# Preparing the third dense weight tile ahead of a branch, loading its raw words over GpSimd's queue, and a scheduling fence at the branch

## The chip, the cores and the metric

The kernel runs on one core of a Trainium2 chip. The metric is the device time of one execution in microseconds (us). The engines are named as in the profile: PE (TensorE's matmuls), PEld (its weight loads), DVE (VectorE), ACT (ScalarE), POOL (GpSimd) and SP (SyncE, which issues most transfers). The letter q behind an engine's name means its sequencer, the part that takes instructions in order.

## What is computed

Three stages follow each other. Attention over 4 batches, 8 heads and 576 positions gives `x` of 2304 tokens by 512. A mixture of 8 experts sends each token to one expert. A dense layer with squared ReLU gives the output:

```python
def _moe_ref(x, w_gate, w_output_gate, w1, w2):
    ...
        h = np.maximum(x[mask] @ w1[e], 0.0)
        ye = h @ w2[e]
        out[mask] = gate_w[mask, None] * eom[mask, e, None] * ye
...
def _moe2_ref(x, w_in, w_out):          # x 2304x512, w_in 512x2048, w_out 2048x512
    h = np.maximum(x @ w_in, 0.0)
    return (h * h @ w_out).astype(np.float32)
```

The dense weights `w_in` and `w_out` arrive as float64. The change concerns only how their first tiles reach the dense layer.

## The kernel before

**Numbers as pairs.** The kernel keeps float32 accuracy on the matmul engine by splitting each operand into a rounded part (hi, type fp32r) and a rest (lo). `mm3` issues three matmuls, hi by hi (L79), hi by lo (L80) and lo by hi (L81), into one accumulator.

**The expert stage** works through units of one or two slots of 128 tokens. Units 0 to 15 (`run(0, NU0)`) always run. Four more units (`run(NU0, NU)`) stand behind a branch, `tc.If(state["used"] > NS0)` (L1065), and run only when routing needs more than 22 slots; in this execution it does not, and they are skipped. Each unit takes four weight chunks `raw0` to `raw3` over SP's queue, ACT and DVE (or POOL) split them into `wc`, PE multiplies, and at the unit's end DVE scales each slot's result into a tile `y` (L975), which SP writes to `y_rest` in device memory (L977). There is one `y` tile only (`YB = 1`), so each scaling waits until the write of the one before it is over.

**The dense stage** takes the 18 token blocks in five groups: four of four blocks and one of two. For each group it runs 16 steps f of 128 hidden columns. Step f does 12 matmuls into `phf` (function `l1`: `x @ w_in`), then ACT's ReLU, square and cast (L1163, L1167, L1169) and DVE's subtraction (L1170) make `gT`, and 12 matmuls per step add `gT @ w_out` into `po` (function `l2`, two steps later in group 0). There are two `phf` buffers.

**The dense weights.** `weights(f)` turns the raw 64-bit words of weight tile f, 128 columns of `w_in` and 128 rows of `w_out`, into hi and lo. Raw words come in two transfers of 512 KB (L1089, L1090). Then ACT takes the absolute value (L1093), a maximum follows (L1094; on DVE for tiles 0 and 1, on POOL for the others), DVE does three integer operations (L1095, L1096, L1097), ACT casts hi (L1098) and DVE subtracts lo (L1100). All 16 tiles are made once, during group 0, and stay. Tiles 0 and 1 (`NPRE = 2`) are made in the expert stage by the generator `dense_prep` (called `ahead`), of which `step(u, place)` takes a piece wherever the table `AH` holds that unit and place. The same generator loads the first four blocks of tokens (`ytp`) and transposes them (`pty`).

**Buffers.** The raw words of tiles 0, 1, 2 and 3 and `ytp` take turns in two buffers of tag `fraw` (`NRAW = 2`); tile 4 and later ones use a place called `spare` as well, which is free only behind the expert stage.

**What sets the order.** In the expert stage the code's order is the order of PE, ACT, DVE and POOL (`manual_schedule`); SP's order and the whole dense stage are set when the program is built, by a scheduler which may also move dense work ahead of the branch when it depends on nothing there. When the branch falls through, SP goes through one semaphore wait for each transfer lane before it continues.

Of the kernel before, what the change touches and what calls it, by code (L numbers as in the profile page):

```python
# [20 lines left out]
P = 128  # L21
# [11 lines left out]
NPRE = 2  # L33
GW = P + 32
NRAW = 2
AH = ((3, 0), (3, 2), (3, 2), (3, 2), (3, 2), (2, 0), (2, 2), (2, 2), (1, 1), (1, 1))
HOLD = 10
LAG = 7
RT0 = 5
# [778 lines left out]
def experts(tc, c, st, x_dram, w1, w2, routed, ahead):  # L818
    nc = tc.nc
    e = st.enter_context  # L820
# [241 lines left out]
        man.close()  # L1062

    run(0, NU0)
    with tc.If(state["used"] > NS0):  # L1065
        run(NU0, NU)


def dense_prep(tc, c, st, w_in, w_out):
    nc = tc.nc  # L1070
    e = st.enter_context
    pre = e(tc.tile_pool(name="pre", bufs=1, side="right", reuse_waits="tile"))
    cv = e(tc.tile_pool(name="cv", bufs=2, side="right", reuse_waits="tile"))
    tiny = 2.0 ** -15
    win32 = w_in.bitcast(I32).rearrange("(k p) (f t) -> p k f t", p=P, t=2)
    wout32 = w_out.bitcast(I32).rearrange("r (f t) -> r f t", t=2)
    c.wi, c.wo = {}, {}
    c.yT = {}

    def weights(f, pool):  # L1080
        w = pool.tile([P, 2, 2, 512], F32R, name=f"w{f}")
        c.wi[f] = w[:, :, 0].rearrange("p t (k q) -> p t k q", k=4)
        c.wo[f] = w[:, :, 1]
        hi, lo = (w[:, t].rearrange("p i q -> p (i q)") for t in range(2))
        raw = c.spare[:, f % 2] if f >= 4 and f & 2 == 0 else cv.tile([P, 2, 512, 2], I32, tag="fraw", name="fraw", bufs=NRAW)
        x = (cv if f < NPRE or f % 2 == 0 else pool).tile([P, 1024], I32, tag="x", name="x", bufs=1)
        xf = x.bitcast(F32)
        with tc.issue_after(c.last) if f < NPRE else nullcontext():
            nc.sync.dma_start(out=raw[:, 0].rearrange("p (k f) t -> p k f t", k=4), in_=win32[:, :, f * P:(f + 1) * P, :])  # L1089
            nc.sync.dma_start(out=raw[:, 1], in_=wout32[f * P:(f + 1) * P])  # L1090
        yield
        lw, hw = (raw.rearrange("p i q t -> p (i q) t")[:, :, t] for t in range(2))
        nc.scalar.activation(xf, hw.bitcast(F32), AF.Abs)  # L1093
        c.pmax = (nc.vector if f < NPRE else nc.gpsimd).tensor_scalar_max(xf, xf, tiny)  # L1094
        nc.vector.tensor_scalar(out=x, in0=x, scalar1=0x07FFFFFF, scalar2=3, op0=ALU.bitwise_and, op1=ALU.logical_shift_left)  # L1095
        nc.vector.scalar_tensor_tensor(out=x, in0=lw, scalar=29, in1=x, op0=ALU.logical_shift_right, op1=ALU.bitwise_or)  # L1096
        nc.vector.scalar_tensor_tensor(out=lw, in0=hw, scalar=-1073741824, in1=x, op0=ALU.bitwise_and, op1=ALU.bitwise_or)  # L1097
        nc.scalar.copy(hi, lw.bitcast(F32))  # L1098
        yield
        nc.vector.tensor_sub(lo, lw.bitcast(F32), hi.bitcast(F32))  # L1100
        yield

    c.weights = weights
    c.yTeven = lambda: pre.tile([P, 2, 4, 4, P], F32R, tag="yT", name="yT")
    yT = c.yT[0] = c.yTeven()
    yt = cv.tile([P, 4, DM], F32, tag="fraw", name="ytp", bufs=NRAW)
    for j in range(2):
        with tc.issue_after(c.last):
            nc.sync.dma_start(out=yt[:, 2 * j:2 * j + 2], in_=c.y_first[2 * j * P:(2 * j + 2) * P].rearrange("(i p) f -> p i f", p=P))
    yield  # L1110
    for j in range(4):
        turn(nc, c, c.bank("pty"), yt[:, j], yT[:, :, j])
        if j % 2:
            yield
    conv = [weights(f, pre) for f in range(NPRE)]
    for g in conv:
        yield from g


def turn(nc, c, pt, src, dst):  # L1120
# [7 lines left out]
def dense(tc, c, st, out):  # L1128
    nc = tc.nc
    e = st.enter_context  # L1130
    dg = e(tc.tile_pool(name="dg", bufs=1, reuse_waits="tile"))
    res = e(tc.tile_pool(name="res", bufs=1, reuse_waits="tile"))
    io = e(tc.tile_pool(name="dio", bufs=2, reuse_waits="tile"))
    hb = e(tc.tile_pool(name="dhb", bufs=2, space=PSUM, reuse_waits="tile"))
    pb = e(tc.tile_pool(name="dpb", bufs=2, space=PSUM, reuse_waits="tile"))
    NF = FF // P
# [42 lines left out]
    for g, (b0, nb) in enumerate(groups):  # L1179
# [4 lines left out]
        gts = {}  # L1184
        lag = 1 if g else 2
        for f in range(NF):
            conv = c.weights(f + 2, res) if g == 0 and NPRE <= f + 2 < NF else iter(())
            next(conv, None)
            gts[f] = l1(g, f)
            for _ in conv:  # L1190
                pass
            if f == HOLD and g == 0:
                hold = c.pmax.ins
            if g < len(groups) - 1:
                if f >= lag:
# [123 lines left out]
```

## Time and profile before

| | us |
|---|---|
| median of 3 runs | 927.83 (927.36 to 929.69) |
| the profiled execution, device time | 928.89 |
| its span, first to last instruction | 927.2 |
| mean granted TensorE clock | 0.993 of full speed |
| PE busy | 900.4 (97%) |
| DVE busy | 579.3 (62%) |
| ACT busy | 469.7 (51%) |
| POOL busy | 228.2 (25%) |

The device time exceeds the span by 1.7 us, which lies outside of the instructions. Attention lasts until about 250 us, the last expert matmul of the profiled execution starts at 508.36 us, the dense stage follows, and its group 0 ends at about 610 us. All times in the rows below count from the span's start.

### The profile page before, as it was taken

The numbers are of one execution on the slowest core, as the hardware profiler recorded it, in microseconds if no ns is written. First come the engines' busy times: TensorE is split into PE (matmuls) and PEld (weight loads), VectorE is DVE, ScalarE is ACT, GpSimd is POOL, SyncE is SP. The second block draws the span as 40 slices with busy tenths as digits, with TensorE's granted clock in tenths as the row PEclk, the third lists the DMA queues.
The fourth block names the chain that finished last, engine by engine and source line by source line (L and its number), as shares of the span: only waits on it lengthen the run. The fifth ranks groups of instructions, "written<-read, shape, count | busy, mean of one in ns | idle before, by whom it ended". The sixth has DMA issues, their size and how long they took to land. (4 is left out here: it accounts for less than half of the span.)

```text
span 927.2 us, 14490 instructions
## 1 busy us (share of the span) xinstructions
PE 900.4 (97%) x5212; PEld 725.1 (78%) x5212; DVE 579.3 (62%) x1080; ACT 469.7 (51%) x934; POOL 228.2 (25%) x275
## 2 busy tenths in 40 slices
PE   7999999999999999999999799999999999999996
PEld 4677777876557889989898587788888888888895
DVE  8789989997686887766677699732223222322332
ACT  5888787864444766565563576622222222322231
POOL 6433433322002142154222345420002000100000
PEclk9999999999999999999999999999999999999998
DMA  9887777745548978766734656110002000100000
GB/s 223 217 196 188 198 197 185 175 110 173 193 149 289 354 279 281 268 226 189 263 122 149 215 182 204 46 58 12 12 12 69 12 12 1 45 1 1 12 35 23
DMA packets 83483, 129.23 MB, mean 139 GB/s; under 512 B 9360, under 2 KB 35984, under 8 KB 83408
## 3 DMA queue, kind: packets, MB, share of 16 engines
q1 hardware_dynamic: 78784, 113.31, 40.2%
q0 software_dynamic: 4624, 14.95, 4.9%
q8 instruction: 43, 0.70, 0.3%
q14 instruction: 32, 0.26, 0.1%
HBM read 109.10 MB, written 15.99 MB: 135 GB/s over the span
## 5 line engine op out<-in xcount | busy, mean ns | idle before, releaser
L1165 DVE SCALAR_TENSOR_TENSOR r<-phf,r 128x512 f32<-128x512 f32 (+1 forms) x64 | 40.0, 625 | 176.2 <-ACT r L1163 176.2
L1163 ACT ACTIVATE r<-phf 128x512 f32<-128x512 f32 (+1 forms) x80 | 44.4, 555 | 196.1 <-PE phf L81 182.3
L852 DVE TENSOR_TENSOR wc<-raw,wc 128x1024 fp32r<-128x1024 f32 x91 | 116.0, 1319 | 12.4 <-ACT wc L850 10.9
L79 PE MATMUL phf<-yT,w 128*128 128x512 f32 (+1 forms) x320 | 121.0, 378 | 2.4 <-ACT w L1098 2.2
L81 PE MATMUL phf<-yT,w 128*128 128x512 f32 (+1 forms) x320 | 119.1, 372 | 0.7 <-DVE w L1100 0.5
L80 PE MATMUL phf<-yT,w 128*128 128x512 f32 (+1 forms) x320 | 117.9, 369 | 0.0
L850 ACT CAST wc<-raw 128x1024 fp32r<-128x1024 f32 x108 | 106.4, 1057 | 20.5 <-DMA raw<-in_w_dram 13.7
L79 PE MATMUL po<-w,gT 128*128 128x512 f32 x256 | 100.6, 394 | 2.6 <-ACT gT L1169 2.6
L80 PE MATMUL po<-w,gT 128*128 128x512 f32 x256 | 99.9, 390 | 0.0
L81 PE MATMUL po<-w,gT 128*128 128x512 f32 x256 | 91.0, 391 | 0.0
L252 ACT ACTIVATE a<-sc,negm 128x512 f32<-128x512 f32 (+3 forms) x128 | 67.0, 532 | 16.8 <-DVE negm L249 16.8
L79 PEld LDWEIGHTS phf<-yT,w 128*128 128x128 f32 x320 | 60.2, 188 | 15.6 <-ACT w L1098 3.9
L81 PEld LDWEIGHTS phf<-yT,w 128*128 128x128 f32 x320 | 60.2, 188 | 13.3 <-DVE w L1100 3.2
L79 PE MATMUL py<-wc,hT 128*128 128x512 f32 x176 | 70.0, 397 | 0.3 <-ACT hT L889 0.3
L80 PE MATMUL py<-wc,hT 128*128 128x512 f32 x176 | 68.9, 391 | 0.8 <-DVE wc L852 0.8
L81 PE MATMUL py<-wc,hT 128*128 128x512 f32 x176 | 68.9, 391 | 0.3 <-DVE hT L890 0.3
L852 POOL TENSOR_TENSOR wc<-raw,wc 128x1024 fp32r<-128x1024 f32 x17 | 44.5, 2621 | 97.0 <-ACT wc L850 88.5
L80 PEld LDWEIGHTS phf<-yT,w 128*128 128x128 f32 x320 | 60.3, 189 | 9.7
L1170 DVE TENSOR_TENSOR gT<-r,gT 128x512 fp32r<-128x512 f32 x64 | 44.2, 691 | 34.2 <-ACT gT L1169 33.4
L249 DVE TENSOR_REDUCE negm<-sc 128x1 f32<-128x512 f32 (+3 forms) x128 | 55.6, 478 | 6.9 <-PE sc L246 6.7
L79 PEld LDWEIGHTS po<-w,gT 128*128 128x128 f32 x256 | 48.1, 188 | 13.7 <-ACT gT L1169 3.5
L1169 ACT CAST gT<-r 128x512 fp32r<-128x512 f32 x64 | 39.7, 621 | 33.4 <-DVE r L1165 33.0
(345 smaller groups left out, 2040.0 us busy)
## 6 DMA issues: line engine op xcount, KB each, us to landing
raw<-in_w_dram SPq DMA_DIRECT2D x64, 1024.0 KB
q<-qh SPq DMA_DIRECT2D x60, 128.0 KB
fraw<-in_w_in_dram SPq DMA_DIRECT2D x10, 512.0 KB
fraw<-in_w_out_dram SPq DMA_DIRECT2D x10, 512.0 KB
kraw<-in_k_dram SPq DMA_DIRECT2D x16, 288.0 KB
qraw<-in_q_dram SPq DMA_DIRECT2D x16, 288.0 KB
y_rest<-y SPq DMA_DIRECT2D x17, 256.0 KB
vts<-in_v_dram SPq DMA_DIRECT2D x16, 256.0 KB
```

The costliest lines, as they stand in the source:

```text
L79: nc.tensor.matmul(out, lhsT=lh, rhs=rh, start=start, stop=False)
L80: nc.tensor.matmul(out, lhsT=lh, rhs=rl, start=False, stop=False)
L81: return nc.tensor.matmul(out, lhsT=ll, rhs=rh, start=False, stop=stop)
L249: nc.vector.tensor_reduce(out=negm[:, h, j:j + 1], in_=psv, axis=AX.X, op=ALU.max, negate=True)
L252: nc.scalar.activation(a[:, h, aoff[j]:aoff[j] + nk], psv, AF.Exp, bias=negm[:, h, j:j + 1], accum_out=ssum[:, h, j:j + 1])
L850: nc.scalar.copy(wc[:, 0, ks], raw[:, ks])
L852: eng.tensor_sub(wc[:, 1, ks], raw[:, ks], wc[:, 0, ks].bitcast(F32))
L1163: nc.scalar.activation(r[:, 0:nt], ph[:, 0:nt], AF.Relu)
L1165: nc.vector.scalar_tensor_tensor(out=r[:, 0:nt], in0=ph[:, 0:nt], scalar=0.0, in1=r[:, 0:nt], op0=ALU.max, op1=ALU.mult)
L1169: nc.scalar.copy(gT[:, 0, 0:nt], r[:, 0:nt])
L1170: nc.vector.tensor_sub(gT[:, 1, 0:nt], r[:, 0:nt], gT[:, 0, 0:nt].bitcast(F32))
```

## The change

Tile 2 is prepared ahead of the branch up to its ACT cast, with the maximum on DVE. The raw words of tiles 0, 1 and 2 and the block load `ytp` go out over GpSimd's queue instead of SP's, and are no longer tied to come after the last chunk load (`issue_after`). The table `AH` has 8 entries instead of 10, which also brings the conversion of tile 1 one place forward. Ahead of the branch what is left of the generator is run, and a fence, `tc.no_sync_barrier()`, keeps the scheduler from moving anything that is written behind it to a place before it. The lines of the dense stage move (L1093 to L1097 become L1092 to L1096, L1098 becomes L1103, L1100 becomes L1105).

```diff
-AH = ((3, 0), (3, 2), (3, 2), (3, 2), (3, 2), (2, 0), (2, 2), (2, 2), (1, 1), (1, 1))
+AH = ((3, 0), (3, 2), (3, 2), (3, 2), (2, 0), (2, 1), (2, 2), (1, 0))
...
     run(0, NU0)
+    for _ in ahead:
+        pass
+    tc.no_sync_barrier()
     with tc.If(state["used"] > NS0):
         run(NU0, NU)
...
-    def weights(f, pool):
-        w = pool.tile([P, 2, 2, 512], F32R, name=f"w{f}")
+    def weights(f):
+        raw = c.spare[:, f % 2] if f >= 4 and f & 2 == 0 else cv.tile([P, 2, 512, 2], I32, tag="fraw", name="fraw", bufs=NRAW)
+        x = (cv if f <= NPRE or f % 2 == 0 else c.res).tile([P, 1024], I32, tag="x", name="x", bufs=1)
+        xf = x.bitcast(F32)
+        eng = nc.gpsimd if f <= NPRE else nc.sync
+        eng.dma_start(out=raw[:, 0].rearrange("p (k f) t -> p k f t", k=4), in_=win32[:, :, f * P:(f + 1) * P, :])
+        eng.dma_start(out=raw[:, 1], in_=wout32[f * P:(f + 1) * P])
+        yield
...
+        c.pmax = (nc.vector if f <= NPRE else nc.gpsimd).tensor_scalar_max(xf, xf, tiny)
...
+        if f == NPRE:
+            yield
+        w = (pre if f < NPRE else c.res).tile([P, 2, 2, 512], F32R, name=f"w{f}")
...
-        with tc.issue_after(c.last):
-            nc.sync.dma_start(out=yt[:, 2 * j:2 * j + 2], in_=c.y_first[2 * j * P:(2 * j + 2) * P].rearrange("(i p) f -> p i f", p=P))
+        nc.gpsimd.dma_start(out=yt[:, 2 * j:2 * j + 2], in_=c.y_first[2 * j * P:(2 * j + 2) * P].rearrange("(i p) f -> p i f", p=P))
+    convs = [weights(f) for f in range(NPRE + 1)]
+    next(convs[0])
...
+    next(convs[2])
+    c.begun = convs[2]
+    yield
...
-            conv = c.weights(f + 2, res) if g == 0 and NPRE <= f + 2 < NF else iter(())
+            conv = iter(()) if g or f + 2 >= NF else c.weights(f + 2) if f + 2 > NPRE else c.begun
```

**SP's queue ahead of the branch.** Before the change its last rows are these; `raw3_3709` is the last expert chunk, `fraw_6455` holds tile 1, `fraw_6933` tile 2 and `fraw_6964` tile 3, and the `y` tiles are the slots of the last two units. A bracket lists the semaphores that an instruction waits for.

```order
L842 DMA raw3_3709<-in_w2_dram 128x4x512 [waits DMAHW6_49,DMAHW1_49,DVE_49]
L1089 DMA fraw_6455<-in_w_in_dram 128x4x256 [waits PE_49]
L1090 DMA fraw_6455<-in_w_out_dram 128x1024 [waits DMAHW3_49]
L1089 DMA fraw_6933<-in_w_in_dram 128x4x256 [waits DMAHW4_49]
L1090 DMA fraw_6933<-in_w_out_dram 128x1024 [waits DMAHW5_49]
L977 DMA y_rest_62<-y_6448 128x512 [waits DVE_49]
L977 DMA y_rest_62<-y_6451 128x512 [waits DMAHW7_49,DVE_49]
L1089 DMA fraw_6964<-in_w_in_dram 128x4x256 [waits DMAHW2_49,DMAHW3_49,DMAHW0_49,DVE_49]
L1090 DMA fraw_6964<-in_w_out_dram 128x1024 [waits DMAHW1_49]
L977 DMA y_rest_62<-y_6516 128x512 [waits DVE_49]
L977 DMA y_rest_62<-y_6519 128x512 [waits DVE_49]
L1065 COMPARE_AND_BRANCH
```

After the change the same stretch reads so:

```order
L842 DMA raw3_3709<-in_w2_dram 128x4x512 [waits DMAHW5_49,DMAHW2_49,DVE_49]
L977 DMA y_rest_62<-y_6463 128x512 [waits DMAHW6_49,DVE_49]
L977 DMA y_rest_62<-y_6466 128x512 [waits DMAHW7_49,DVE_49]
L977 DMA y_rest_62<-y_6525 128x512 [waits DVE_49]
L977 DMA y_rest_62<-y_6528 128x512 [waits DMAHW1_49,DVE_49]
L1088 DMA fraw_6964<-in_w_in_dram 128x4x256 [waits DMASW3_49,DMASW4_49,DMASW0_49,DMASW7_49,PE_49,Activation_49]
L1089 DMA fraw_6964<-in_w_out_dram 128x1024 [waits DMAHW3_49]
L1068 COMPARE_AND_BRANCH
```

The loads of tiles 1 and 2 have left this queue, and the load of tile 3 has moved from ahead of the last two `y` writes to behind them; it now stands directly at the branch.

**ACT behind the branch.** Before the change, from the last two casts of expert weights to the second ReLU, ACT's rows are these; `phf_6937` is step 0 and `phf_6968` step 1.

```order
L850 CAST wc_6850<-raw3_3709 128x1024 [waits DMAHW0_49,DVE_49,Pool_49]
L850 CAST wc_6850<-raw3_3709 128x1024
L1065 UNCONDITIONAL_BRANCH
L1065 UNCONDITIONAL_BRANCH [waits Activation_49]
L1163 ACTIVATE r_6950<-phf_6937 128x512 [waits DMASW6_49,DMASW5_49,DMASW7_49,DMASW2_49,PE_49]
L1098 CAST w2_6932<-fraw_6933 128x1024 [waits DMAHW2_49,DVE_49,Activation_49]
L1093 ACTIVATE x_6965<-fraw_6964 128x1024 [waits DMAHW0_49,DVE_49,DMAHW1_49,PE_49,DMAHW3_49,Activation_49,Pool_49]
L1167 ACTIVATE r_6950<-r_6950 128x512 [waits Activation_49]
L1169 CAST gT_6953<-r_6950 128x512 [waits DMASW3_49,DMASW4_49,DMASW1_49,DMASW6_49,DMASW0_49,Activation_49]
L1093 ACTIVATE x_6995<-spare_6927 128x1024 [waits DMAHW5_49,DMAHW4_49]
L1163 ACTIVATE r_6981<-phf_6968 128x512 [waits DVE_49]
```

After the change (`phf_6944` is step 0, `fraw_6329` tile 2):

```order
L850 CAST wc_6860<-raw3_3709 128x1024 [waits DMAHW0_49,DVE_49,Pool_49]
L850 CAST wc_6860<-raw3_3709 128x1024
L1068 UNCONDITIONAL_BRANCH
L1068 UNCONDITIONAL_BRANCH [waits Activation_49]
L1103 CAST w2_6942<-fraw_6329 128x1024 [waits DVE_49,DMAHW2_49,PE_49,Activation_49]
L1092 ACTIVATE x_6965<-fraw_6964 128x1024 [waits DVE_49,DMAHW3_49,Activation_49,Pool_49]
L1181 ACTIVATE r_6957<-phf_6944 128x512 [waits DMASW5_49,PE_49]
L1185 ACTIVATE r_6957<-r_6957 128x512 [waits Activation_49]
L1187 CAST gT_6960<-r_6957 128x512 [waits DMASW4_49,DMASW3_49,Activation_49]
L1092 ACTIVATE x_6995<-spare_6937 128x1024 [waits DMAHW5_49,DMAHW4_49]
L1181 ACTIVATE r_6981<-phf_6968 128x512 [waits DVE_49,PE_49]
```

The first ReLU (`r_6957<-phf_6944`) stood first behind the branch; it now stands third, behind the absolute value of tile 3 (`x_6965<-fraw_6964`), which waits for tile 3's raw words (the lane DMAHW3).

**DVE ahead of the branch.** After the change its last rows are these; `x_6257` is tile 1 and `x_6330` tile 2. Before the change the order was `wc`, the first two `y`, all of tile 1, a `y`, tile 2 without its maximum, the last `y`.

```order
L852 TENSOR_TENSOR wc_6434<-raw3_3709,wc_6434 128x1024 [waits DMAHW5_49,Activation_49]
L975 TENSOR_SCALAR y_6463<-py_6333,fsel_4250 128x512 [waits DMAHW4_49,PE_49]
L975 TENSOR_SCALAR y_6466<-py_6334,fsel_4250 128x512 [waits DMAHW6_49,DVE_49,PE_49]
L1105 TENSOR_TENSOR w1_6431<-fraw_6256,w1_6431 128x1024
L1093 TENSOR_SCALAR x_6330<-x_6330 128x1024 [waits Activation_49]
L1094 TENSOR_SCALAR x_6330<-x_6330 128x1024 [waits DVE_49]
L1095 SCALAR_TENSOR_TENSOR x_6330<-fraw_6329,x_6330 128x1024 [waits DMASW2_49,DMASW1_49,DVE_49]
L1096 SCALAR_TENSOR_TENSOR fraw_6329<-fraw_6329,x_6330 128x1024 [waits DVE_49]
L975 TENSOR_SCALAR y_6525<-py_6475,fsel_4250 128x512 [waits DMAHW7_49,PE_49]
L975 TENSOR_SCALAR y_6528<-py_6476,fsel_4250 128x512 [waits DMAHW0_49,DVE_49,PE_49]
L1068 COMPARE_AND_BRANCH
```

Both last `y` scalings now follow the whole of tile 2.

## Rows read from the trace of the kernel before

**Rows 1.** The page: first line, and busy us of each engine.

```profile
span 927.2 us, 14490 instructions
...
PE 900.4 (97%) x5212; PEld 725.1 (78%) x5212; DVE 579.3 (62%) x1080; ACT 469.7 (51%) x934; POOL 228.2 (25%) x275
```

**Rows 2.** Waits of PE from 430 us on: us in total, times, longest.

```profile
PE po L79 <- ACT gT L1169: 2.6, 2, 1.8
PE phf L79 <- ACT w L1098: 2.2, 2, 1.9
PE phf L81 <- DVE w L1100: 0.5, 1, 0.5
```

**Rows 3.** Windows: length, busy of PE PEld DVE ACT POOL, clock, DMA, GB/s.

```profile
533.00:553.00 20.00, 20.00 (x90) 16.52 (x89) 19.82 (x18) 13.67 (x18) 11.15 (x4) 1.00 0.52 178
...
573.00:593.00 20.00, 19.49 (x87) 14.47 (x86) 19.23 (x20) 12.77 (x18) 13.35 (x6) 1.00 0.31 101
...
613.00:900.00 287.00, 287.00 (x1338) 237.97 (x1337) 83.07 (x130) 72.94 (x131) 23.06 (x23) 1.00 0.06 22
```

**Rows 4.** Timeline of PE: start, us, what, [idle before <- releaser].

```profile
515.60 0.50 PE L79 MATMUL phf<-yT,w 128*128 128x512 f32 x1 [1.86 <-ACT w L1098]
...
516.86 0.50 PE L81 MATMUL phf<-yT,w 128*128 128x512 f32 x1 [0.53 <-DVE w L1100]
```

**Rows 5.** Timeline of ACT around the branch; columns as in rows 4.

```profile
513.87 0.60 ACT L1163 ACTIVATE r<-phf 128x512 f32<-128x512 f32 x1 [8.23 <-PEq L1065]
...
515.45 1.15 ACT L1093 ACTIVATE x<-fraw 128x1024 f32<-128x1024 f32 x1
...
520.98 1.13 ACT L1093 ACTIVATE x<-spare 128x1024 f32<-128x1024 f32 x1 [3.20 <-DMA spare<-in_w_out_dram]
```

**Rows 6.** Timeline of SP's queue (x2: from first to last issue).

```profile
506.30 0.50 SPq L1090 DMA_DIRECT2D fraw<-in_w_out_dram  x1
...
506.85 6.66 SPq L977 DMA_DIRECT2D y_rest<-y  x2
...
515.77 0.39 SPq L1089 DMA_DIRECT2D spare<-in_w_in_dram  x1
```

**Rows 7.** Windows behind the load issued at 506.30; columns as in rows 3.

```profile
508.40:511.00 2.60, 2.60 (x13) 2.17 (x12) 2.37 (x3) 0.00 (x0) 0.13 (x1) 1.00 0.96 344
...
511.00:511.50 0.50, 0.50 (x4) 0.42 (x3) 0.50 (x1) 0.00 (x0) 0.00 (x0) 1.00 0.53 189
...
511.50:512.00 0.50, 0.50 (x4) 0.38 (x3) 0.28 (x1) 0.00 (x0) 0.00 (x0) 1.00 0.10 37
```

**Rows 8.** Chain that ended last, a piece from 500 to 540 us.

```profile
516.21 4.69 DMA spare<-in_w_out_dram
```

**Rows 9.** Timeline of POOL and DVE: tile 4 and the pace.

```profile
522.19 2.77 POOL L1094 TENSOR_SCALAR x<-x 128x1024 f32<-128x1024 f32 x1 [2.75 <-ACT x L1093]
...
525.68 0.69 DVE L1095 TENSOR_SCALAR x<-x 128x1024 int32<-128x1024 int32 x1
...
538.87 2.06 DVE L1096 SCALAR_TENSOR_TENSOR x<-fraw,x 128x1024 int32<-128x1024 int32 x1
...
544.55 2.07 DVE L1096 SCALAR_TENSOR_TENSOR x<-fraw,x 128x1024 int32<-128x1024 int32 x1
```

**Rows 10.** Timeline of DVE ahead of the branch, two y tiles.

```profile
498.83 0.75 DVE L975 TENSOR_SCALAR y<-py,fsel 128x512 f32<-128x512 f32 x1 [2.89 <-DMA y_rest<-y]
...
512.40 0.75 DVE L975 TENSOR_SCALAR y<-py,fsel 128x512 f32<-128x512 f32 x1 [0.62 <-DMA y_rest<-y]
```

**Rows 11.** Timeline of PE, SP and POOL: ytp, and two POOL rows.

```profile
473.07 1.91 PE L75 MATMUL pty<-ident,ytp 128*128 128x128 f32 x16
...
443.33 1.06 SPq L1109 DMA_DIRECT2D ytp<-y_first  x2
...
458.07 0.57 POOL L980 DMA_DIRECT2D y_rest<-y  x1 [3.35 <-DVE y L975]
...
578.73 3.81 POOL L1094 TENSOR_SCALAR x<-x 128x1024 f32<-128x1024 f32 x1 [2.90 <-ACT x L1093]
```

More of the change, by code (lines that the diff above doesn't have):

```diff
@@ L1078, in dense_prep @@
     c.yT = {}
-    def weights(f, pool):
-        w = pool.tile([P, 2, 2, 512], F32R, name=f"w{f}")
+    def weights(f):
[6 more added lines that the diff above has]
+        yield
+        lw, hw = (raw.rearrange("p i q t -> p (i q) t")[:, :, t] for t in range(2))
+        nc.scalar.activation(xf, hw.bitcast(F32), AF.Abs)
+        c.pmax = (nc.vector if f <= NPRE else nc.gpsimd).tensor_scalar_max(xf, xf, tiny)
+        nc.vector.tensor_scalar(out=x, in0=x, scalar1=0x07FFFFFF, scalar2=3, op0=ALU.bitwise_and, op1=ALU.logical_shift_left)
+        nc.vector.scalar_tensor_tensor(out=x, in0=lw, scalar=29, in1=x, op0=ALU.logical_shift_right, op1=ALU.bitwise_or)
+        nc.vector.scalar_tensor_tensor(out=lw, in0=hw, scalar=-1073741824, in1=x, op0=ALU.bitwise_and, op1=ALU.bitwise_or)
+        if f == NPRE:
+            yield
+        w = (pre if f < NPRE else c.res).tile([P, 2, 2, 512], F32R, name=f"w{f}")
         c.wi[f] = w[:, :, 0].rearrange("p t (k q) -> p t k q", k=4)
@@ L1084, in weights @@
         hi, lo = (w[:, t].rearrange("p i q -> p (i q)") for t in range(2))
[L1085 to L1097, printed above, removed]
         nc.scalar.copy(hi, lw.bitcast(F32))
@@ L1114, in dense_prep @@
             yield
-    conv = [weights(f, pre) for f in range(NPRE)]
-    for g in conv:
-        yield from g
+    next(convs[1])
+    next(convs[0])
+    yield
+    for _ in convs[0]:
+        pass
+    next(convs[2])
+    yield
+    next(convs[1])
+    yield
+    for _ in convs[1]:
+        pass
+    yield
+    next(convs[2])
+    c.begun = convs[2]
+    yield
 def turn(nc, c, pt, src, dst):
@@ L1131, in dense @@
     dg = e(tc.tile_pool(name="dg", bufs=1, reuse_waits="tile"))
-    res = e(tc.tile_pool(name="res", bufs=1, reuse_waits="tile"))
+    res = c.res = e(tc.tile_pool(name="res", bufs=1, reuse_waits="tile"))
     io = e(tc.tile_pool(name="dio", bufs=2, reuse_waits="tile"))
```

## Prediction

> **What bounds the kernel now.** I read the page first. PE is busy for 900.4 of 927.2 us [rows 1], so only PE's idle time can be won, and anything that lets PE idle longer is lost. The view of waits then says where PE waits for another engine in the stretch that the change touches: from 430 us to the end there are only three entries, 2.6, 2.2 and 0.5 us, together 5.3 us [rows 2], all in the dense stage. So the change has nothing to win in the expert stage, where no wait of PE is listed after 430 us, and at most 5.3 us behind it.
>
> The timeline of PE shows the part of this that belongs to tile 2: step f=2 of the dense stage starts at 515.60 after 1.86 us of waiting for ACT's cast of tile 2, and at 516.86 PE waits 0.53 us more for its lo half [rows 4]. These 2.4 us are what an earlier tile 2 aims at. The other 2.6 us are waits for `gT` a few microseconds later.
>
> The windows view says what sets the pace after that. From 533 to 553 us DVE is busy for 19.82 of 20 us, and from 573 to 593 still for 19.23, with PE full too [rows 3]. The same DVE instruction, L1096, recurs from 538.87 to 544.55, a period of 5.68 us [rows 9]. A step needs 24 matmuls of PE, which at 90 in 20 us [rows 3] is 5.3 us. So from step 6 or so until tile 15 is converted the conversions on DVE set the pace, and a delay that reaches DVE at 525 us finds no gap to be given back in. From 613 to 900 us PE is full and DVE busy for only 83 of 287 us [rows 3]: a shift that has reached the end of group 0 reaches the end of the program.
>
> **The change, part by part.**
>
> *Tile 2 ahead of the branch.* Its absolute value, maximum and three integer operations now lie in the last expert units, where PE is full. ACT and DVE have room there, and DVE's part ends only about as late as the old order did, since in both cases the last y scaling (512.40 before [rows 10]) is what comes last. The cast of tile 2 comes first on ACT behind the branch, so hi is there at about 515.0 at the latest, if nothing else holds step 2. This removes up to 1.86 + 0.53 = 2.4 us of idle time, but only if step 2 can start.
>
> *Tile 3's load behind the fence.* This is the edit that decides, I think. Before, SP issued tile 3's second transfer at 506.30, ahead of the last two `y` writes, which occupy the queue from 506.85 for 6.66 us, to 513.51 [rows 6]. It landed under the last matmuls of the expert stage: the DMA share is 0.96 until 511.0, 0.53 in the next half microsecond and 0.10 in the one after [rows 7], so the load was over at about 511.6, 5.3 us after its second issue. ACT read it only at 515.45 [rows 5]; it was early by 4 us. After, the fence puts both transfers behind the last `y` write. The writes themselves depend on the y scalings, and these come at about the old time (two scalings follow each other at the pace of the writes between them: at 498.83 DVE had waited 2.89 us for one [rows 10]; if both intervals are that long it is 1.3 us later, if they are quick it is the old time). So the first transfer is issued at about 513.5, the second at 513.95 (the spacing of rows of this kind is 0.4 to 0.5 us), and it lands 4.69 us later, as the spare load issued at 516.21 did [rows 8], or 5.3 us later, as this same load did before: 518.7 to 519.3. I take 519.2, since it is the same transfer right behind a write.
>
> *ACT's order behind the branch.* ReLU of step 0 ran at 513.87 before, first of all [rows 5]. Now it stands behind the absolute value of tile 3, which waits for that landing. So ACT does the cast of tile 2, waits from 515 to 519.2, takes 1.15 us for the absolute value [rows 5] and 0.60 us for the ReLU [rows 5], which ends at about 520.9. Only then is one of the two `phf` buffers free for step 2. PE has done steps 0 and 1 by about 513.7 (515.60 less its wait of 1.86 [rows 4]) and stands until about 520.9, where it started step 2 at 515.60 before: 5.3 us later, and its idle time grows from 2.4 to about 7 us. Some of this comes back at once, because the two waits for `gT` (2.6 us [rows 2]) are swallowed by it. So PE by itself would be late by 2 to 3 us at step 4.
>
> *Tile 4's load.* SP leaves the branch only when all its transfers have landed. Before, it issued the load of tile 4 at 515.77 [rows 6], ACT took its absolute value at 520.98 on its landing [rows 5]. Now SP is held by tile 3's load until about 519.3 and issues at about 519.5: 3.8 us later, and so are the absolute value and POOL's maximum, which ended at 522.19 + 2.77 = 524.96 and now ends at 528.7 [rows 9]. DVE took it up at 525.68, that is 0.72 us after it was there [rows 9], so DVE is late by 3.8 − 0.7 = 3.1 us. From here the chain of DVE is without gaps, and this stays.
>
> *DVE's work in group 0.* Tile 2's maximum moves from POOL to DVE, 0.7 us in a place where DVE has room. At the tail of group 0 one L1095 of the last tile (0.69 us [rows 9]) comes ahead of the lo half of the tile before. I count half of it, 0.35 us.
>
> *GpSimd's queue.* The transfers of `ytp`, tiles 0, 1 and 2 leave SP. `ytp` was issued at 443.33 and is used first at 473.07 [rows 11]; now it stands behind POOL's write of 458.07 [rows 11], and still has 15 us. I cost this at nothing. What hides it is the distance to 473; without it, each microsecond of lateness is one of PE.
>
> The Trainium skill ("SBUF — State Buffer", section "SBUF: two separate sides") warns of just this: a transfer issued from GpSimd has its descriptors written by GpSimd, and while DVE holds the port pair that the two share they cannot be written, so that plain loads belong on SP or ACT. This kernel's only sign of such sharing is one maximum on POOL that took 3.81 us [rows 11] where most take 2.77 [rows 9]. By the row the delay is a microsecond, and nothing; by the rule it could be several, and this is the last rival below.
>
> *Sum.* 3.1 us at tile 4, kept by a full DVE, and 0.35 at the tail: 3.45 us. The profiled execution has a span of 927.2 and a device time of 928.89; the median of three is 927.83, 1.1 less. On the span it gives 930.65, on the profiled time 932.3, on the median 931.3, and I take **931.3 us**. Between the ends of its unknown costs (landing in 4.69 or 5.3 us, the y scalings at the old time or 1.3 us later, the extra L1095 at nothing or 0.69) it is 930.4 to 932.9.
>
> The page "DMA: Bandwidth & Descriptors" of the Trainium skill (section "Anatomy of one DMA — SWDGE (gpsimd) path") gives 2.0 us and the bytes at 436 GB/s, so for the two transfers of 1 MB together an estimate of 4.4 us, where the row has 4.69; by it the sum would be some 0.9 us less than mine.
>
> **The rivals.**
>
> *Absorbed.* The load is exposed, but less of it arrives: the last y scaling comes earlier than 512.40, since the tiles are already converted, or the load lands in 4 us, or ACT's wait overlaps what SP waits for anyway (before, SP came out of the branch only at 515.77 [rows 6]). For it speaks that a y scaling waits only for PE and for the write before it. Against it: that scaling already came at 512.40 with 0.62 us of waiting for a write [rows 10], and nothing behind it is quicker than it was. With 1.5 to 2 us off the landing the sum is 1 to 2.5 us: 928.8 to 930.4.
>
> *Faster.* The load of tile 3 does not matter: if its absolute value were not in front of the ReLU, or if it landed by 515, then tile 2 being ready removes PE's 2.4 us [rows 4], and DVE, free of tile 2's lo half until later, starts tile 3 earlier: 925.4; at the floor of all three waits, 5.3 us [rows 2], 922.5. It decides if tile 3's raw words are there before about 515.5, the time at which ACT read them before [rows 5]. That needs an issue ahead of about 510, and the order puts it behind a write that was issued at 513.
>
> *GpSimd's queue late.* If descriptors wait for DVE, or POOL's own subtractions are held up, `ytp` or a tile comes late at 473, or the last expert chunk at 503. With 3 to 5 us on top of the forecast it is 934 to 936. It decides if `ytp` lands after 473.07. DVE is busy for most of the stretch, but no load of the trace shows such a wait.
>
> **How the numbers follow.** Forecast 0.55, absorbed 0.27, faster 0.07, GpSimd's queue 0.11. A measurement tells this kernel from no change at about 0.3%, 2.8 us, so "slower" starts at 930.6. Of the forecast 0.48 lies beyond it and 0.07 within, all of the absorbed case is within, GpSimd's is slower (0.11), of the faster case 0.06 is beyond 925.0 and 0.01 not: faster 0.06, same 0.35, slower 0.59. The range for 8 in 10 leaves out the faster case, and half of the one with GpSimd's queue late: 928.8 to 935.0. The likeliest case's own range is 930.4 to 932.9.
>
> **What would show it.** Right: in the timeline of SP the load of tile 3 is issued at 513 to 515 behind the last `y` write; ACT's absolute value of tile 3 waits 3 to 5 us for that DMA, and the ReLU of step 0 follows it at about 520; PE's wait list shows 5 to 7 us for ACT's ReLU or its `phf` buffer where it had 1.9 for the cast of tile 2; the absolute value of tile 4 comes at 524 to 525; the last lo half of group 0 and the end are later by the same 3 to 4 us; `pty` is not later than 473. Wrong: if PE starts step 2 before 518, if DVE has idle time between 530 and 590 that takes the delay up, or if PE waits ahead of the branch.

## The result

| | before | after |
|---|---|---|
| median, us | 927.88 (4 runs) | 934.09 (933.33 to 935.57, 4 runs) |
| span of the profiled execution | 927.2 | 932.7 |
| ratio | | 1.0064 (95% interval 1.0047 to 1.0080) |

The change makes the kernel 6.2 us slower. The forecast was 3.45 us slower, 931.3 us; direction and mechanism held, the size did not. The measured time lies within the range for 8 in 10 (928.8 to 935.0) and above the likeliest case's own (930.4 to 932.9).

The page of the changed kernel, its first line and the busy times that answer to [rows 1]:

```profile
span 932.7 us, 14491 instructions
...
PE 900.1 (97%) x5212; PEld 727.0 (78%) x5212; DVE 582.4 (62%) x1081; ACT 469.1 (50%) x934; POOL 232.3 (25%) x282
```

PE has the same work, and the span is 5.5 us longer, so PE lost time somewhere. Its waits from 430 us on, as in [rows 2]:

```profile
PE phf L79 <- ACT r L1181: 7.3, 1, 7.3
PE phf L81 <- DVE w L1105: 2.5, 3, 1.3
PE phT L81 <- POOL wc L852: 0.4, 1, 0.4
```

One wait of 7.3 us for ACT's ReLU has come in the place of those for the cast of tile 2 (2.2 us) and for `gT` (2.6 us). The second entry was one wait of 0.5 us; it is now three waits for lo halves, 2.5 us, in the middle of group 0. The timeline of PE shows the first wait where step 2 starts:

```profile
521.11 0.80 PE L79 MATMUL phf<-yT,w 128*128 128x512 f32 x1 [7.33 <-ACT r L1181]
```

Step 2 starts at 521.11, where it started at 515.60 before [rows 4]. The reason is in SP's queue (timeline; the first row holds four issues):

```profile
501.26 12.56 SPq L977 DMA_DIRECT2D y_rest<-y  x4
514.04 0.39 SPq L1088 DMA_DIRECT2D fraw<-in_w_in_dram  x1
514.48 0.57 SPq L1089 DMA_DIRECT2D fraw<-in_w_out_dram  x1
519.76 0.38 SPq L1088 DMA_DIRECT2D spare<-in_w_in_dram  x1
```

Tile 3's two transfers, issued by 506.30 before [rows 6], go out at 514.04 and 514.48, directly behind the last `y` write, and tile 4's first transfer follows at 519.76, 4.0 us later than before. What SP does in between is the branch (instructions of line L1068 on SP's sequencer; duration in ns, first and last start in us):

```profile
L1068 SPq EVENT_SEMAPHORE  x9: 17/17/17, 515.3 to 519.6; - x9
...
L1068 SPq COMPARE_BRANCH  x1: 53/53/53, 515.1 to 515.1; - x1
```

SP entered the branch at 515.1 and went through nine semaphore instructions, one lane after the other, until 519.6. In the kernel before, where tile 3's load was over at about 511.6 [rows 7], the same nine took 1.5 us:

```profile
L1065 SPq EVENT_SEMAPHORE  x9: 17/17/17, 514.1 to 515.6; - x9
```

ACT hangs on these. Its timeline behind the branch, against [rows 5]:

```profile
518.00 1.11 ACT L1103 CAST w<-fraw 128x1024 fp32r<-128x1024 f32 x1 [16.69 <-SPq L1068]
519.35 1.23 ACT L1092 ACTIVATE x<-fraw 128x1024 f32<-128x1024 f32 x1 [0.24 <-SPq L1068]
520.48 0.57 ACT L1181 ACTIVATE r<-phf 128x512 f32<-128x512 f32 x1
...
524.91 1.19 ACT L1092 ACTIVATE x<-spare 128x1024 f32<-128x1024 f32 x1 [2.54 <-DMA spare<-in_w_out_dram]
```

Note the bracket of the first row: even the cast of tile 2, whose words had been ready since 509, was released only by SP's sequencer at 518.00. Then come the absolute value of tile 3, the first ReLU at 520.48 (513.87 before), and tile 4's absolute value at 524.91 (520.98 before). DVE's timeline shows the y scalings, which the y writes wait for, and what DVE made of tile 4:

```profile
500.49 0.75 DVE L975 TENSOR_SCALAR y<-py,fsel 128x512 f32<-128x512 f32 x1
503.40 0.75 DVE L975 TENSOR_SCALAR y<-py,fsel 128x512 f32<-128x512 f32 x1 [2.17 <-DMA y_rest<-y]
...
509.06 0.74 DVE L975 TENSOR_SCALAR y<-py,fsel 128x512 f32<-128x512 f32 x1
512.72 0.75 DVE L975 TENSOR_SCALAR y<-py,fsel 128x512 f32<-128x512 f32 x1 [2.92 <-PE phf L81]
...
529.38 0.69 DVE L1094 TENSOR_SCALAR x<-x 128x1024 int32<-128x1024 int32 x1 [0.76 <-POOL x L1093]
```

The last y scaling starts at 512.72, the last expert matmul at 507.54 (in the kernel before 512.40 [rows 10] and 508.36). So counted from PE's end of the expert stage, the scaling is 1.1 us later. Its bracket names a matmul of the dense stage, on which it does not depend; it reads `py` and needs the one `y` buffer, so the write of the `y` tile ahead of it is the likelier releaser. DVE takes up tile 4 at 529.38, which was 525.68 [rows 9]. Last, the windows, columns as in [rows 3], of the change:

```profile
521.10:523.00 1.90, 1.89 (x5) 1.51 (x6) 0.60 (x1) 1.23 (x2) 1.90 (x1) 0.50 0.97 313
...
525.00:527.00 2.00, 2.00 (x6) 1.52 (x6) 1.68 (x2) 1.97 (x3) 0.83 (x1) 0.50 1.05 390
527.00:529.00 2.00, 2.00 (x10) 1.66 (x9) 0.69 (x1) 1.97 (x4) 2.00 (x1) 0.97 1.09 378
553.00:573.00 20.00, 17.52 (x74) 13.21 (x74) 18.67 (x16) 12.48 (x16) 11.70 (x4) 1.00 0.48 161
```

And of the kernel before:

```profile
521.00:525.00 4.00, 2.19 (x11) 1.47 (x10) 1.50 (x3) 3.12 (x5) 2.77 (x1) 1.00 1.07 383
...
553.00:573.00 20.00, 19.96 (x86) 15.55 (x85) 19.80 (x19) 14.08 (x18) 10.13 (x5) 1.00 0.60 206
```

Behind its wait PE runs at a granted clock of 0.50, that is 1.2 GHz, until about 527; before, it was 1.00 there. And from 553 to 573 PE is busy for 17.52 us where it was 19.96.

### The profile page after: what moved, and what is told of

Same layout as the page of the kernel before. It is cut to its first block, busy times and chain, and to the rows that moved or that the text cites. A ratio compares the mean times of both kernels' runs of the same rounds, so it can differ in the third digit from the quotient of the medians.

```text
span 932.7 us, 14491 instructions
## 1 busy us (share of the span) xinstructions
PE 900.1 (97%) x5212; PEld 727.0 (78%) x5212; DVE 582.4 (62%) x1081; ACT 469.1 (50%) x934; POOL 232.3 (25%) x282
## 5 line engine op out<-in xcount | busy, mean ns | idle before, releaser
L852 DVE TENSOR_TENSOR wc<-raw,wc 128x1024 fp32r<-128x1024 f32 x91 | 118.3, 1342 | 15.1 <-ACT wc L850 13.6
L1234 POOL DMA_INDIRECT out_dram<-ob,rtok x13 | 12.7, 973 | 184.1 <-DVE ob L1233 160.3
```

The lines of the kernel that those rows point to most:

```text
L852: eng.tensor_sub(wc[:, 1, ks], raw[:, ks], wc[:, 0, ks].bitcast(F32))
L1234: nc.gpsimd.indirect_dma_start(out=out, out_offset=bass.IndirectOffsetOnAxis(ap=c.tok[b0 + j], axis=0), in_=ob, in_offset=None)
```

## The experiments

Two theories. **A**: the fence puts tile 3's load behind the y writes; this holds SP in the branch, and through SP, ACT, PE and tile 4's load. **B**: the loads on GpSimd's queue and the added work on DVE cost the time. A third, **C**, was formed on the way: tile 2's conversion on DVE delays the last `y` scalings, and with them SP's way out of the branch. Each ratio is to the kernel before, run on the same chip in the same session (median 929.0 for the first four runs, 928.8 for the next four, 928.3 and 929.4 for the others).

| run | median, us | ratio, 95% interval |
|---|---|---|
| the change | 934.09 | 1.0064 (1.0047 to 1.0080) |
| 1 no fence | 930.59 | 1.0021 (1.0009 to 1.0034) |
| 2 tile 3's load ahead | 931.43 | 1.0034 (1.0023 to 1.0046) |
| 3 the same, ReLU first | 930.53 | 1.0016 (1.0007 to 1.0026) |
| 4 ReLU first alone | 934.57 | 1.0061 (1.0042 to 1.0079) |
| 5 run 3, tile 2 behind the y's | 932.78 | 1.0051 (1.0031 to 1.0071) |
| 6 tile 2 behind the y's alone | 934.90 | 1.0063 (1.0049 to 1.0078) |
| 7 queue alone | 935.89 | 1.0074 (1.0059 to 1.0088) |
| 8 fence alone | 934.17 | 1.0062 (1.0047 to 1.0077) |
| 9 run 3, old order of the y's | 929.68 | 1.0016 (1.0006 to 1.0026) |
| 10 run 9 on SP's queue | 929.52 | 1.0013 (1.0003 to 1.0023) |
| 11 filler matmuls in the change | 942.35 | 1.0142 (1.0124 to 1.0159) |
| 12 filler matmuls in run 2 | 936.63 | 1.0079 (1.0065 to 1.0094) |

**Run 1, the fence left out.**

```diff
-    tc.no_sync_barrier()
     with tc.If(state["used"] > NS0):
```

> The change with only its scheduling fence left out; tile 3's load then goes out ahead of the last two y writes again, and ACT's first ReLU stands ahead of the absolute value of tile 3. Theory A (tile 3's load, pushed behind the y writes by the fence, holds SP in the branch, and with it ACT, PE and tile 4's load): PE starts step 2 at 515 to 516.5 instead of 521.1, no 7.3 us wait, clock stays at 1.00, tile 4's load is issued at about 515.5, and the time falls back to 927 to 929 us. Theory B (the loads on GpSimd's queue and the extra work on DVE cost it): the wait goes but 2 us or more stay, 931 to 934 us.

Measured: of 0.64%, 0.21% stay, so 4.0 us go (0.43% of 928). SP's timeline:

```profile
505.91 0.39 SPq L1087 DMA_DIRECT2D fraw<-in_w_in_dram  x1
506.35 0.50 SPq L1088 DMA_DIRECT2D fraw<-in_w_out_dram  x1
510.32 3.56 SPq L977 DMA_DIRECT2D y_rest<-y  x2
516.13 0.38 SPq L1087 DMA_DIRECT2D spare<-in_w_in_dram  x1
```

Tile 3 is loaded at 505.91 again, and tile 4's load goes out at 516.13. So A names the larger part. But 1.9 us stay, more than A allowed: 930.59 us lies between A's range and B's. PE still waited 3.8 us for the first ReLU, and its granted clock was 0.50 from 515 to 521, neither of which A expected.

**Run 2, the fence kept and only tile 3's load written ahead of it** (the tile `x` is therefore taken one step later, behind the load).

```diff
-    convs = [weights(f) for f in range(NPRE + 1)]
+    convs = [weights(f) for f in range(NPRE + 2)]
...
     for _ in convs[1]:
         pass
+    next(convs[3])
...
-    c.begun = convs[2]
+    c.begun = convs[2:]
```

> The change with the fence kept and only tile 3's raw load written ahead of it, behind tile 1's conversion. SP's order is that of the kernel without the fence, but ACT's first ReLU now stands behind the absolute values of tiles 3 and 4, and tile 4's load can only be issued behind the branch. Theory A1 (the place of tile 3's load on SP is all that counts): 927 to 929 us. Theory A2 (what counts as well is that the first ReLU stands behind a load that lands late): ReLU at about 522, PE idle for 8 us or more before step 2, but tile 4's conversion on time on DVE, so that DVE's chain is not late and most of it is given back: 929.5 to 932 us. Theory B: 931 to 934 us.

Measured: 0.34% above before, 931.43 us, inside A2's range of 929.5 to 932 and also inside B's of 931 to 934, so that the trace has to decide. PE's waits and ACT's timeline:

```profile
PE phf L79 <- ACT r L1182: 8.9, 1, 8.9
```

```profile
520.60 1.14 ACT L1092 ACTIVATE x<-spare 128x1024 f32<-128x1024 f32 x1 [4.47 <-DMA spare<-in_w_out_dram]
521.65 0.57 ACT L1182 ACTIVATE r<-phf 128x512 f32<-128x512 f32 x1
```

PE stands for 8.9 us, longer than in the change itself, because the first ReLU now waits behind tile 4's absolute value, and yet this costs less: tile 4 is at 520.60, 13.5 us behind the last expert matmul (507.10), against 12.6 before and 17.4 in the change. This is what A2 had described. With DVE nearly on time, 8.9 us of standing still cost 3.2 us; in the change, 7.3 us and a late DVE cost 6.

**Run 3, the same with ACT's order tied.**

```diff
-        nc.scalar.activation(xf, hw.bitcast(F32), AF.Abs)
+        with tc.issue_after(c.act0[f - NPRE - 1]) if f in (NPRE + 1, NPRE + 2) else nullcontext():
+            nc.scalar.activation(xf, hw.bitcast(F32), AF.Abs)
...
+        if not g and not f:
+            c.act0 = relu, cast
```

> As the run before, and ACT's first ReLU held ahead of the absolute value of tile 3 and its cast ahead of that of tile 4. Theory A in both forms: PE starts step 2 at 515 to 516.5, 927 to 929 us, the same as without the fence. Theory B: 931 to 934 us.

Measured: 0.16%, 930.53 us, again between the two theories' ranges, and the same as without the fence within the intervals. So beyond what it does to tile 3's load and to ACT's order, no cost of the fence can be seen. A rest of about 1.5 us stays here too.

**Run 4, ACT's order alone**, with the diff of run 3 in the change as it is.

> The change with fence and late load of tile 3 kept, and only ACT's order changed: the first ReLU ahead of the absolute value of tile 3. If the ReLU's place behind that load is what holds PE: step 2 starts at 515 to 516, and PE has done its work by the time DVE needs it; tile 4 is still late, 930 to 932 us. If ACT is held by SP in the branch anyway (the cast of tile 2 ahead of the ReLU started at 518.0, when SP's semaphore waits of the branch had come to its lane): step 2 starts at 519.5 to 520, only 1.3 us earlier, and the time is 932.5 to 934 us.

Measured: 0.61%, no gain. ACT's timeline:

```profile
517.90 1.11 ACT L1104 CAST w<-fraw 128x1024 fp32r<-128x1024 f32 x1 [16.36 <-SPq L1068]
518.91 0.59 ACT L1182 ACTIVATE r<-phf 128x512 f32<-128x512 f32 x1
```

The second expectation holds in kind, though the time is 0.6 us above its range: the cast of tile 2, ahead of the ReLU, is itself released by SP's sequencer at 517.90. The ReLU's place behind tile 3 was not the bar; SP's stay in the branch was. Nothing of the 1.6 us by which the ReLU came earlier reached the end. DVE took up tile 4 hardly sooner (21.7 us behind the last expert matmul, 21.8 in the change, 17.3 before), and PE waited 2.3 us for a block of tokens later.

**Runs 5 and 6, tile 2's conversion behind the last y scalings**, in run 3 and in the change.

```diff
-AH = (..., (2, 2), (1, 0))
+AH = (..., (2, 2), (1, 2))
```

> The third run (tile 3's load ahead of the fence, the first ReLU ahead of tile 3's absolute value) with one entry of the table changed, (1, 2) for (1, 0): tile 2's conversion comes behind the last two y scalings on DVE, not ahead of them. Theory C (what stayed of the loss, 1 to 2 us, is that tile 2's conversion delays the last two y scalings by 1 us, with them SP's way out of the branch, tile 4's load and DVE's chain): the last y scaling comes at about 509 instead of 512 to 515, SP issues tile 4's load 2 to 3 us earlier than in the kernel before, and the time is 1 to 2.5 us below the kernel before. Theory B (it is the loads on GpSimd's queue): unchanged, 1 to 2 us above it.

> The change as it is with only that entry of the table changed, (1, 2) for (1, 0). The last two y writes then go out at 507 to 510, and tile 3's load, which now stands behind the branch on SP, goes out at about 512 to 513 and lands at 517 to 518; the first ReLU still stands behind tile 3's absolute value. Theory A with C: step 2 starts at 519 to 520, tile 4's load is issued at about 513, so DVE's chain is not late, and the loss falls from 6 us to 1 to 3. If tile 3's load and the ReLU behind it are all that counts: 4 to 5 us stay.

Measured: 0.51% and 0.63%, that is 4.0 and 6.1 us above the kernel before; both expectations of C failed, and the figures of the rivals (1 to 2 us in run 5, 4 to 5 in run 6) were missed as well. The timeline of DVE in run 5, and of ACT:

```profile
504.28 0.75 DVE L975 TENSOR_SCALAR y<-py,fsel 128x512 f32<-128x512 f32 x1 [2.17 <-DMA y_rest<-y]
...
508.62 0.75 DVE L975 TENSOR_SCALAR y<-py,fsel 128x512 f32<-128x512 f32 x1 [2.46 <-DMA y_rest<-y]
513.15 0.75 DVE L975 TENSOR_SCALAR y<-py,fsel 128x512 f32<-128x512 f32 x1 [3.78 <-DMA y_rest<-y]
```

```profile
517.97 1.11 ACT L1104 CAST w<-fraw 128x1024 fp32r<-128x1024 f32 x1 [15.79 <-DVEq L1068]
```

Two things went otherwise. The last y scaling did not come at 509 but at 513.15: it waited 3.78 us for the write before it, which went out beside tile 3's load, and the scaling before had waited 2.46 us for its own. And tile 2's conversion, now behind it, ended at 517.75, so that the cast could not start before 517.97 (the bracket names DVE's sequencer at the branch). In run 6 tile 3's load went out only at 516.16, 7.6 us behind the last expert matmul, where it was 6.5 in the change.

**Run 7, the queue alone**: the kernel before with GpSimd's queue for `ytp` and tiles 0 and 1, which are no longer tied to the last chunk load.

```diff
-        with tc.issue_after(c.last) if f < NPRE else nullcontext():
-            nc.sync.dma_start(out=raw[:, 0]..., in_=win32[...])
-            nc.sync.dma_start(out=raw[:, 1], in_=wout32[...])
+        eng = nc.gpsimd if f < NPRE else nc.sync
+        eng.dma_start(out=raw[:, 0]..., in_=win32[...])
+        eng.dma_start(out=raw[:, 1], in_=wout32[...])
```

> The kernel before with only the queue changed: the block load and the raw words of tiles 0 and 1 go out over GpSimd's queue, not tied to the last chunk load. Theory A or C: no difference, within 1 us of the kernel before. Theory B: 1.5 us or more above it, with waits of PE for a late block load or a late tile ahead of the branch.

Measured: 0.74% above before, which looked like B. The timeline of POOL, and of ACT:

```profile
485.73 2.50 POOL L852 TENSOR_TENSOR wc<-raw,wc 128x1024 fp32r<-128x1024 f32 x1 [16.55 <-ACT wc L850]
496.68 2.43 POOL L852 TENSOR_TENSOR wc<-raw,wc 128x1024 fp32r<-128x1024 f32 x1 [8.45 <-ACT wc L850]
499.06 0.79 POOL L1089 DMA_DIRECT2D fraw<-in_w_in_dram  x1
499.84 0.57 POOL L1090 DMA_DIRECT2D fraw<-in_w_out_dram  x1
```

```profile
505.19 1.12 ACT L1093 ACTIVATE x<-fraw 128x1024 f32<-128x1024 f32 x1 [8.64 <-DMA fraw<-in_w_out_dram]
```

The loss comes from an order, not from a slow queue. Tile 1's load stands on POOL behind the subtraction of the last expert chunk, which waits for that chunk until 496.68; so it is issued at 499.06 where SP had issued it at 490. It lands 5.35 us after its second issue (499.84 to 505.19), against 4.75 us on SP before (490.53 to 495.28). In the change the new table takes tile 1's load one place earlier, ahead of that subtraction, and it went out at 474. The change needs its table for its queue.

**Run 8, the fence alone** in the kernel before.

```diff
     run(0, NU0)
+    for _ in ahead:
+        pass
+    tc.no_sync_barrier()
```

> The kernel before with only the fence. Tile 2's raw load then stands behind the last y write too, and tile 3's behind it; tile 2 is converted wholly behind the branch. Theory A: tile 2's second transfer is issued at about 514.5 and lands at 519 to 520, its conversion (1.15 + 2.8 + 3.2 + 1.1 us) ends at 527 to 528, PE starts step 2 there instead of at 515.6, its clock falls meanwhile, and the time is 8 to 12 us above the kernel before. If the fence costs nothing by itself: no difference.

Measured: 0.62%, 5.4 us, less than the 8 to 12 of A. Tile 2's load was issued at 509 and not at 514: with no conversion between them, the last two y scalings came at 504.97 and 507.86. The rest of the expectation held in kind, tile 2's conversion lay behind the branch.

**Runs 9 and 10, the old order of the y scalings.** Run 3 with three entries of the table moved; run 10 besides with every load on SP's queue (where the scheduler, which sets SP's order, issued `ytp` and tile 0 as early as 273 to 311 us).

```diff
-AH = (..., (3, 2), (2, 0), (2, 1), (2, 2), (1, 0))
+AH = (..., (3, 2), (2, 0), (2, 2), (1, 0), (1, 2))
```

> The third run (fence kept, tile 3's load ahead of it, first ReLU ahead of tile 3's absolute value) with three entries of the table moved: tile 1's conversion comes behind the y scalings of the last unit but one, as in the kernel before, and tile 2's behind those of the last unit. The fifth run had put only tile 2's there, and its last y scaling still came at 513, since the four scalings wait for each other's writes and the first of them stood behind tile 1's conversion. Theory C (what stays of the loss is this chain of y scalings and writes, which holds SP in the branch and tile 4's load): first scaling back at about 495, the last at 509 to 510, tile 4's load issued at 513 to 514 instead of 518, DVE's chain 1 to 2 us ahead of the kernel before, and a time 0 to 2.5 us below it. Theory B (the loads on GpSimd's queue cost the rest): still 1 to 2 us above the kernel before.

> As the run beside it, with all loads on SP's queue instead of GpSimd's. Theory C: the same time as that run within 1 us. Theory B: 1 to 2 us faster than that run.

Measured: 0.16% and 0.13%. Run 9 alone would have fitted B's 1 to 2 us; run 10 decides, since the time hardly changes without GpSimd's queue. The medians differ by 0.2 us. The traces show what the queue does cost, in the longest of three instructions named DRAIN on POOL's sequencer, at the end of the program (duration in ns, shortest, median and longest; first run 9, then run 10):

```profile
L1338 POOLq DRAIN  x3: 50/109/6757, 919.9 to 927.2; - x3
```

```profile
L1338 POOLq DRAIN  x3: 50/109/6097, 920.9 to 927.5; - x3
```

At the end of the program this drain takes 6.76 us with the eight transfers on GpSimd's queue and 6.10 without, and the other engines' last instructions follow it; in the change it is 6.76, in the kernel before 6.11. So the queue costs 0.65 us, not B's 1 to 2, and that half of B falls. The added work on DVE, B's other half, is not isolated by any run. C's gain did not come either. DVE and SP of run 9:

```profile
493.42 0.75 DVE L975 TENSOR_SCALAR y<-py,fsel 128x512 f32<-128x512 f32 x1
...
504.30 0.75 DVE L975 TENSOR_SCALAR y<-py,fsel 128x512 f32<-128x512 f32 x1 [0.96 <-PE py L81]
509.59 0.75 DVE L975 TENSOR_SCALAR y<-py,fsel 128x512 f32<-128x512 f32 x1 [4.54 <-DMA y_rest<-y]
```

```profile
505.07 5.62 SPq L977 DMA_DIRECT2D y_rest<-y  x2
514.40 0.38 SPq L1086 DMA_DIRECT2D spare<-in_w_in_dram  x1
```

```profile
L1068 SPq EVENT_SEMAPHORE  x9: 17/17/17, 510.9 to 512.7; - x9
...
L1068 DVEq EVENT_SEMAPHORE  x1: 21/21/21, 514.2 to 514.2; - x1
```

The last rows are of line L1068 as above. The last scaling waited 4.54 us for a write beside tile 3's load. SP was through its own semaphores at 512.7, and still issued tile 4's load only at 514.40, right behind DVE's passing at 514.2: DVE had tile 2's conversion to do ahead of the branch. In this execution the last expert matmul starts at 506.59, so tile 4's load at 514.40 is 7.8 us behind it; before it was 515.77 − 508.36 = 7.4. It is not earlier. In run 3 it was 8.4 us behind. With this, tile 4 is taken up by DVE no sooner than before (18.0 us behind the last expert matmul, against 17.3), and an early tile 2 has nothing to give.

**Runs 11 and 12, matmuls that nobody reads, in PE's long wait.** They ask whether the half clock costs time.

```diff
+        if not g and f == 1:
+            pt = pb.tile([P, 512], F32, tag="tr", name="pty")
+            with tc.issue_after(mm.ins):
+                for i in range(28):
+                    c.fill = nc.tensor.matmul(pt, lhsT=wi[0][:, 0, 0], rhs=yT[:, 0], start=True, stop=True).ins
```

> The change with 28 matmuls added that are read by nobody, between PE's steps 1 and 2, where it stands for 7.3 us; at 0.227 us each they fill 6.3 us. In the changed kernel PE ran at a granted clock of 0.50 from 521 to 527 us, behind that wait, and 12 matmuls took 5.5 us instead of 2.7. If the clock is part of the loss: it stays at 1.00 and the time falls by 2 to 3 us below the change. If DVE's conversions set the end whatever PE's clock was: step 4 starts at most 0.7 us earlier (its weights' lo half is there 0.7 us before PE takes it), and the time stays within 0.7 us of the change.

> The second run (tile 3's load ahead of the fence, the first ReLU behind tiles 3 and 4) with 34 such matmuls in its wait of 8.9 us. There DVE's conversions were on time (the last lo half 0.8 us earlier behind the last expert matmul than in the kernel before) and PE was late by 2.9 us at step 4. If PE's late start and its clock were its loss: the clock stays at 1.00, step 4 starts 2.5 us earlier, and the time falls by 2 to 3 us, to that of the kernel before or below it. If not: unchanged, 2.5 to 3 us above the kernel before.

Measured: by the ratios 0.8 and 0.45% slower than the kernels they were added to, some 7 and 4 us, outside both expectations. The windows and one row of PE's timeline in run 11:

```profile
514.00:518.00 4.00, 4.00 (x19) 3.33 (x18) 0.00 (x0) 0.59 (x1) 0.00 (x0) 1.00 0.86 289
...
522.00:526.00 4.00, 4.00 (x19) 3.13 (x17) 3.52 (x4) 1.64 (x3) 1.24 (x2) 1.00 1.06 391
580.00:600.00 20.00, 15.38 (x56) 11.90 (x57) 16.41 (x16) 11.93 (x17) 6.76 (x2) 0.83 0.02 7
```

```profile
590.65 0.80 PE L81 MATMUL po<-w,gT 128*128 128x512 f32 x1 [2.89 <-DVE gT L1194]
```

The clock did stay at 1.00 where it had been 0.50, from 521 to 527; it fell to 0.50 later, from about 530 to 533 and from 588 to 595. But the scheduler, which orders the dense stage by its own model of time, took the added matmuls into account and ordered DVE's work of group 0 anew: a `gT` came to stand behind integer operations that wait for POOL, and PE stood for 2.89 us near the end of the group (and 1.7 us just ahead, for ACT's cast of a `gT`). In run 12 the clock was 1.00 up to 540 as well, and PE stood twice for 2.1 us on a `gT`. The runs changed more than one thing, and what the half clock costs stays open.

## Why the prediction was right in direction and short in size

**Tile 3's load decides: right.** It was said to be issued at 513.5 and 513.95 and to land at 518.7 to 519.3; it was issued at 514.04 and 514.48, and ACT read it at 519.35, at most 4.87 us behind the second issue and so between the two rows' 4.69 and 5.3. The estimate of 4.4 us from the Trainium skill ("DMA: Bandwidth & Descriptors", section "Anatomy of one DMA — SWDGE (gpsimd) path") rests on a fit that the page gives for transfers issued from GpSimd; this load went over SP's queue. Runs 1 and 3 show its share: with the load and ACT's order back in place, 4.0 and 4.5 us are gone (0.64% less 0.21% and 0.16%, of 928).

**"These come at about the old time" (the last y scalings): mis-sized.** This is the step that failed first. I had the other bound, 1.3 us later, and did not take it; measured, from the last expert matmul, it is 1.1 us. The prediction looked at the last scaling alone. All four hang on each other's writes, and the first of them had gone from 495.19 to 500.49 behind tile 1's conversion.

**"Hi is there at about 515.0 at the latest": wrong.** The cast waited until 518.00, for SP's sequencer. I had SP's wait in the branch hold only SP's next load. Run 4 shows that it holds ACT as well, since with the ReLU put first the cast still came at 517.90. This alone did not change the sum, since the ReLU had been put at 520.3 for another reason; it came at 520.48. That it came out so well is luck: ACT was to wait 4 us for tile 3's words behind the cast, and waited for SP ahead of the cast instead, only 0.24 us behind it.

**DVE late by 3.1 us at tile 4: mis-sized.** 529.38 against 525.68 [rows 9] is 3.7, and since the expert stage ended 0.8 us earlier in this execution (507.54 against 508.36), 4.5 us from there. The y scalings make 1.1 of the 1.4 us of difference.

**The delay that DVE keeps: right, but not all of it.** Run 3 shows it most plainly: DVE took up tile 4 18.49 us behind the last expert matmul, against 17.32 before, and its last lo half still ended 1.2 us later (89.4 against 88.2). In the change the whole from the last expert matmul to the end of the span is 425.11 us against 418.81, 6.3 longer. 4.5 us are there at tile 4, and 0.65 us are POOL's longer drain at the end. The other 1.1 us come in the middle of group 0, where PE was busy for 17.52 of 20 us from 553 to 573, with 2.5 us of waits for lo halves. The order of DVE's work there was made anew with the change; I had counted one instruction of it, 0.35 us. That PE can lose several microseconds there without DVE being later is seen in run 11, where DVE's last lo half was earlier than in the change, 90.3 against 92.9 us behind the last expert matmul, and the end 6.9 us later.

**GpSimd's queue, costed at nothing: mis-sized by 0.65 us.** What the prediction looked at held: `ytp` was not late, and `pty` came at 472.05 where it had come at 473.07 [rows 11]. The price stands at the end of the program, in POOL's drain. The Trainium skill ("SBUF — State Buffer", section "SBUF: two separate sides") warns that a transfer issued from GpSimd can be held up while DVE holds the ports that the two share. Run 7's rows can't test this, since DVE was busy there for only 0.75 of the 6.20 us from 499.00 to 505.20. In the trace of the change DVE was busy for 6.67 of the 6.70 us from 487.80 to 494.50; tile 2's second transfer, issued by GpSimd at 488.63, landed 4.5 us later, no later than the 4.75 us over SP's queue in the kernel before. So no run here shows that delay; which of DVE's instructions hold the shared ports, the rows don't say.

**The range.** That 934.09 us lies inside the range for 8 in 10 is partly luck. What the range had above 932.9 was there for GpSimd's queue being late ahead of the branch, and that did not happen.

**What an early tile 2 gives: nothing.** Runs 3, 9 and 10 have it with tile 3's load in place, and all three are 0.13 to 0.16% slower than before. The likeliest reason, argued and not shown: from tile 4 on DVE sets the pace, and tile 4's load waits for the last engine to pass the branch, which more work ahead of the branch can only delay. Of the 1.2 to 1.5 us that stay in these runs, DVE's last lo half accounts for 0.8 to 1.2 (89.0 to 89.4 us behind the last expert matmul against 88.2), and in runs 3 and 9 POOL's drain for 0.65; these sums lie within the runs' intervals. No version beat the kernel before.

## What to carry to other kernels

In this kernel SP waited in the branch for the transfer that was under way when it came there (until 519.6 us, against 512.7 in run 9, where the load had gone out ten microseconds earlier), and ACT's work behind the branch waited with it: look at what is issued last ahead of a branch before looking at what is computed there. Where one engine paces a later stage, ask what an earlier start does to that engine's first bound instruction, here tile 4 on DVE; that nothing else counts is not shown, since in run 2 PE's late start cost 3 us with DVE nearly on time. A fence costs what it keeps from moving: list every load that the scheduler had carried across that place. And a queue may have a price far from where it is used: look at the end of the program too.

## What had not been expected of the hardware

PE's granted clock was 0.50 (1.2 GHz) from 521 to about 527 us, after a wait of 7.3 us, and 12 matmuls took 5.5 us; in the kernel before it was 1.00 behind a wait of 1.9 us, and in run 11, with the wait filled, 1.00 in the same stretch. It was 0.50 behind run 2's wait of 8.9 us and behind run 1's of 3.8 us as well. A 256 KB write that shared the DMA engines with a load of 1 MB kept the next y scaling waiting 4.54 us (run 9), where the first write of the same trace had kept one waiting 2.16. POOL's drain at the end of the program took 6.11 us in the kernel before, 6.60 with six more transfers on GpSimd's queue (run 7) and 6.76 with eight more (the change).
